# A transformer block on one core: two x tiles on ScalarE's queue, low parts on VectorE or GpSimd, and places for single operations

## The chip, the cores and the metric

The kernel is one program on one core of a Trainium2 chip. The metric is the device time of an execution in microseconds (us). The engines are TensorE (PE; its weight loads are listed as PEld), VectorE (DVE), ScalarE (ACT), GpSimd (POOL) and SyncE (SP), which here only issues DMA transfers.

## The reference

Two layers, each added to its input, on 2048 tokens of width 448, in float32:

```python
def layer_1(x, wqkv, wo):                 # S = 2048, D = 448, H = 16 heads of 28
    q, k, v = split(layernorm(x) @ wqkv)
    scores = einsum("bhqd,bhkd->bhqk", q, k) * 28 ** -0.5
    mask = (i - j >= 0) & (i - j < 256)   # each query sees itself and the 255 before it
    p = softmax(where(mask, scores, -1e9))
    return x + einsum("bhqk,bhkd->bhqd", p, v) @ wo

def layer_2(h, w_gate, w_up, w_down):     # 448 -> 1792 -> 448
    n = layernorm(h)
    return h + (gelu(n @ w_gate) * (n @ w_up)) @ w_down
```

## The kernel before

**Precision.** Each matrix operand of a projection is held as a high part, made on ScalarE (`to_hi`, line 467), and a low part, the rest, made by a subtraction on VectorE or GpSimd (`to_lo`, line 470). A product is three passes of TensorE: high by high, high by low, low by high.

**Layer 1.** The tokens are 16 tiles of 128 (`hres`, loaded at line 603). A tile is normalised (statistics at lines 493 and 495, the norm itself at 545 on VectorE, 522 on ScalarE or 541 on GpSimd), turned by TensorE (line 527) and split into parts (`xT`). Values are made at line 683, queries and keys at line 721; the scores at 831, their row maxima with the mask on VectorE (895), the exponentials on ScalarE (901, into `pp`), the triangle of the mask on GpSimd (907). Line 983 multiplies by the values; the sums are drained by ScalarE (467) and VectorE (1021 to 1023), and the output projection is line 1048, with its weights `wo` loaded at lines 1062 and 1069 and split like the others. Tiles 8 to 15 are turned through DRAM (570, 579, 581).

**Layer 2.** The gate and up products use a Strassen-like scheme: sums of weights are made by `weight_set` (lines 1368 for sums, 467 and 470 for their parts), the products are line 1509, and their results leave PSUM by a copy on ScalarE or VectorE (`copied`, lines 1515 and 1516) and by additions on VectorE (`added`, 1521). A part of it is done in the plain way at lines 1296 and 1308. The second half is line 1585, with weights from `down_set`, added to `hres` at line 1605. In its first half a `seen` (1422 on ScalarE, 1423 on VectorE) reads one element of a PSUM bank, so that the order of the banks is kept.

**Order.** Nothing is scheduled by the compiler. The code adds operations to `Lists`, each with an engine, a cost, a latency and a key; `Lists.run` then plays them through a model of the engines and writes every engine's program in the order in which it started them. At each step it takes, among operations that can start at nearly the same time, the one with the smallest key. The table `PLACE` adds a number to the keys of a unit: "k6" is the split of a set of query and key weights, "ws4" a weight set of layer 2, "q", "v", "o" projections, "s", "m", "p", "a" the stages of attention, "ln" norms, "tx" parts of the normalised tokens, "ds" a set of down weights. Some operations may run on either of two engines (`alts`); the loop chooses.

**DMA.** All loads before are issued by SP's queue in one order. The model of a transfer has one bus that all share. At the start the four first x tiles go out, then the two halves of the first value weights (`pp`, line 662), then the first query and key weights (`raw`, line 692). TensorE fills the wait with transposes of nothing (line 1883) until data is there.

Of the kernel before, what the change touches and what calls it, by code (L numbers as in the profile page):

```python
# [116 lines left out]
}  # L117
HAND = {}
# [11 lines left out]
class Op:  # L130
    __slots__ = ("eng", "cost", "lat", "key", "fn", "deps", "users", "left", "banks", "port", "ready", "start", "fin", "unit", "name",
                 "size", "tag", "mode", "alts", "then", "soft")
# [9 lines left out]
class Lists:  # L142
# [3 lines left out]
    def __init__(self):  # L146
        self.ops, self.seen, self.open, self.all, self.unit = [], {}, {}, {}, None
        self.free_ones = {}

    def op(self, eng, cost, lat, key, fn, r=(), w=(), bank=None, port=False, size=0, tag=None, after=(), part=None, mode=0, alts=None):  # L150
# [10 lines left out]
        o.key, o.unit = key + PLACE.get(self.unit, 0), self.unit  # L161
# [37 lines left out]
    def run(self, allowed, idle):  # L199
# [65 lines left out]
        while n:  # L265
# [28 lines left out]
            if e == "sp":  # L294
                bus = max(bus, t + 1.2) + o.size * (0.003 if t < 15 else 0.0034) + {2: 1.0, 3: 0.5}.get(len(dmas), 0)
                lat = bus + 0.7 - t
                dmas.append(t + lat)
# [1656 lines left out]
```

## Time and profile before

| | |
|---|---|
| time, median of 3 runs | 678.3 us (677.99 to 679.79) |
| the profiled execution | 677.47 us, of which the span 675.8 us |
| TensorE busy | 668.2 us (99%) |
| VectorE busy | 532.1 us (79%) |
| ScalarE busy | 361.9 us (54%) |
| GpSimd busy | 201.8 us (30%) |
| granted clock of TensorE | full in nearly every slice |

Busy time of an engine is what it spent in instructions, as a share of the span. Matmuls are pipelined, so that two of them overlap in the timeline, and a group's time is read from the start of one group to the start of the next. Lines are those of the kernel before; in the changed kernel the same code stands 121 to 123 lines further down.

### The profile page before, as it was taken

To read this page: it belongs to the slowest core of one execution; us is meant where nothing else is said; L and a number is where in the kernel's file an instruction comes from. 1 tells how busy PE (TensorE), PEld (TensorE's weight loads), DVE (VectorE), ACT (ScalarE), POOL (GpSimd) and SP (SyncE) were. 2 spreads that over 40 slices of the span, in tenths; PEclk is the share of its full clock that TensorE was granted. 3 is DMA by queue.
4 is the path that set the end of the run, shared out by engine and by line. 5 is a ranking of instruction groups with operands and counts; after the bars stand their busy time and mean duration, and the time that the engine had idled before them with its cause. 6 is when DMAs were issued, how large, how long until landed. Compare 5 with 4: busy or idle time off the path is not lost.

```text
span 675.8 us, 21887 instructions
## 1 busy us (share of the span) xinstructions
PE 668.2 (99%) x8673; PEld 560.5 (83%) x8673; DVE 532.1 (79%) x1613; ACT 361.9 (54%) x788; POOL 201.8 (30%) x392
## 2 busy tenths in 40 slices
PE   8999999999999999999999999999999999999997
PEld 7887778777877676788888988888899999899887
DVE  8977887977788789469978899668568878887745
ACT  4748777565655475645554475643534445546430
POOL 5125755655555464822121131200000110000000
PEclk9999999999999999999999999999999999999999
DMA  8333231112203265108663964425014734543103
GB/s 300 103 80 85 50 69 46 35 34 64 66 9 68 79 211 179 34 1 222 139 148 93 240 187 143 127 77 157 8 32 129 235 111 128 146 147 89 44 15 110
DMA packets 76678, 71.61 MB, mean 106 GB/s; under 512 B 50080, under 2 KB 64608, under 8 KB 76000
## 3 DMA queue, kind: packets, MB, share of 16 engines
q1 hardware_dynamic: 76432, 70.10, 37.3%
q8 instruction: 68, 1.11, 0.7%
q14 instruction: 34, 0.28, 0.2%
q10 hardware_dynamic: 144, 0.11, 0.0%
HBM read 59.87 MB, written 23.36 MB: 123 GB/s over the span
## 4 chain that ended last, share of the span: by engine, by line
PE 94%; DMA 2%; DVE 1%; ACT 1%; issue 0%; POOL 0%; DVEq 0%; SPq 0%; ACTq 0%
PE bank L1509 27%; PE bank L1585 19%; PE bank L831 11%; PE bank L721 11%; PE bank L1296 7%; PE bank L1048 6%; PE bank L683 6%; PE bank L983 6%; PE bank L1308 2%; DMA proj<-down 1%; PE bank L1621 1%; DMA raw<-in_wo_dram 1%; PE bank L527 0%; DMA hres<-in_x_dram 0%; ACT pp L901 0%
## 5 line engine op out<-in xcount | busy, mean ns | idle before, releaser
L895 DVE CUSTOM_DVE_ANT_0 mt<-bank,mt 128x192 bf16<-128x192 f32 (+4 forms) x368 | 115.1, 373 | 23.3 <-PE bank L831 20.8
L1509 PE MATMUL bank<-xT,proj 64*128 64x512 f32 x645 | 116.7, 389 | 0.2 <-ACT raw L1515 0.2
L907 POOL TENSOR_SCALAR_AFFINE_SELECT pp<-pp 64x256 f32<-64x256 f32 x240 | 96.9, 425 | 58.8 <-ACT pp L901 53.9
L1509 PE MATMUL bank<-xo,proj 64*128 64x512 f32 x456 | 93.1, 388 | 0.4 <-DVE e L1423 0.4
L901 ACT ACTIVATE pp<-bank 128x512 f32<-128x512 f32 x152 | 79.1, 597 | 23.2 <-PE bank L831 23.1
L1509 PEld LDWEIGHTS bank<-xT,proj 64*128 64x128 f32 x645 | 75.5, 184 | 7.5 <-ACT raw L1515 0.6
L721 PE MATMUL bank<-xT 128*128 128x512 f32 x308 | 79.8, 402 | 0.0
L1585 PE MATMUL bank<-proj,gh 64*128 64x448 f32 x624 | 72.1, 362 | 0.0
L721 PEld LDWEIGHTS bank<-xT 128*128 128x128 f32 x308 | 55.4, 188 | 16.1 <-ACT pp L901 2.3
L1585 PEld LDWEIGHTS bank<-proj,gh 64*128 64x128 f32 x624 | 61.3, 184 | 5.0 <-ACT e L1422 0.2
L1509 PEld LDWEIGHTS bank<-xo,proj 64*128 64x128 f32 x456 | 55.7, 184 | 5.7 <-DVE e L1423 0.8
L1509 PE MATMUL bank<-xT,w 64*128 64x512 f32 x276 | 51.1, 388 | 0.0
L1605 DVE TENSOR_TENSOR hres<-bank,hres 128x448 f32<-128x448 f32 (+1 forms) x85 | 47.4, 609 | 2.4 <-PE bank L1621 1.9
L831 PE MATMUL bank<-k,q 28*64 28x320 f32 (+4 forms) x1544 | 46.9, 338 | 0.5 <-ACT pp L901 0.3
L1509 PE MATMUL bank<-xo,w 64*128 64x512 f32 x240 | 46.5, 391 | 0.2
L831 PE MATMUL bank<-q,k 29*64 29x320 f32 (+4 forms) x1472 | 43.7, 350 | 0.0
L683 PE MATMUL bank<-proj,xT 128*128 128x448 f32 (+1 forms) x220 | 43.0, 337 | 0.4 <-ACT proj L467 0.3
L831 PEld LDWEIGHTS bank<-q,k 29*64 29x64 f32 x1472 | 27.3, 131 | 18.3 <-issue 7.3
L683 PEld LDWEIGHTS bank<-proj,xT 128*128 128x128 f32 x220 | 35.5, 189 | 5.4 <-issue 1.0
L831 PEld LDWEIGHTS bank<-k,q 28*64 28x64 f32 x1544 | 35.4, 131 | 5.1 <-DVE mx L895 1.3
L983 PE MATMUL bank<-pp,v 64*29 64x192 f32 (+4 forms) x1472 | 38.6, 340 | 0.6 <-ACT pp L901 0.6
L1296 PE MATMUL bank<-xT,proj 64*128 64x512 f32 x312 | 37.8, 390 | 0.0
(200 smaller groups left out, 1275.1 us busy)
## 6 DMA issues: line engine op xcount, KB each, us to landing
gu<-in_gu_dram SPq DMA_DIRECT2D x18, 480.0 KB
proj<-gu SPq DMA_DIRECT2D x24, 288.0 KB
proj<-down SPq DMA_DIRECT2D x22, 224.0 KB
proj<-gu SPq DMA_DIRECT2D x24, 192.0 KB
hres<-in_x_dram SPq DMA_DIRECT2D x16, 224.0 KB
w<-gu SPq DMA_DIRECT2D x12, 288.0 KB
out_dram<-hres SPq DMA_DIRECT2D x15, 224.0 KB
xT<-xn SPq DMA_DIRECT2D x26, 128.0 KB
```

Source lines behind the costliest of these rows:

```text
L683: op("pe", mm(224 * n), 0.29 if n == 1 else 0.38, key + a / 16, lambda a=a, h=h, wb=wb, xb=xb: nc.tensor.matmul(bank[b.k][:, 0:224 * n], x ...
L721: op("pe", mm(512) + 0.002, 0.403, key, lambda a=a, h=h, wb=wb, xb=xb: nc.tensor.matmul(bank[b.k], wqk[m][:, h, wb, :], xT[:, xb, cc * 128 ...
L831: nc.tensor.matmul(bank[banks[j].k][dst, at:at + 64 * n], w, x, start=True, stop=True, tile_position=(32 * j, 64 * h), skip_group_check=True)
L895: nc.vector.tensor_tensor_reduce(junk[turn_of[0]][:, 0:x], bank[b.k][:, 64 * o:64 * o + x], mask[:, lo:lo + x], 1.0, -BIG, OP.add, OP.max, ...
L901: op("act", 0.065 + width * 0.00088, 0.16 + width * 0.00088, key, lambda: nc.scalar.activation(pp[:, j, at:at + width], bank[b.k][:, 0:wid ...
L907: nc.gpsimd.affine_select(a, a, pattern=[[0, 4], [-cm, 64]], compare_op=op_, fill=0.0, base=0, channel_multiplier=cm)
L983: nc.tensor.matmul(bank[banks[h].k][32 * j:32 * j + DH + 1, 64 * lo:64 * hi], v[HALF[h], at_v(4 * c - 2 + kh // 2), 4 * g + j, :], pp[HALF ...
L1048: op("pe", mm(D), 0.38, wk, lambda a=a, h=h, oh=oh, wh=wh, i=i, k=k: nc.tensor.matmul(bank[k.k][:, 0:D], ohl[h][oh][:, i * 128:(i + 1) * 1 ...
L1296: nc.tensor.matmul(bank[banks[side ^ ph].k], cwbuf[n % 4][0]()[HALF[side], o:o + 128], carea(c, xl, j, side), start=not ph and not j and n ...
L1509: nc.tensor.matmul(bank[b.k], w, xarea(u.cp, xl, xs, side)[:, xk], start=p in (1, 2, 5) and not k and not t, stop=t == 2, tile_position=(6 ...
L1585: nc.tensor.matmul(bank[banks[q].k][:, 0:D], h[oh][0]()[HALF[x], q * 128:q * 128 + 128], d[wh][0]()[HALF[x]], start=not ph and not y and n ...
L1605: op("dve", 0.07 + w * 0.463 / D, 0.163 + w * 0.463 / D, key, lambda: nc.vector.tensor_tensor(hres[:, t, c0:c0 + w], bank[b.k][:, c0:c0 + ...
```

## The change

The changed kernel computes the same with the same number of matmuls. It has five parts. (1) Tiles 2 and 3 of x are loaded by ScalarE's DMA queue in place of SP's; the planner is told that they follow the identity matrix, though no instruction waits for it. (2) The low parts of the value weights and of the query and key weights may run on VectorE or on GpSimd. (3) `PLACE` grows from 163 entries to 866, of which 709 name a single operation ("q0.2:13" is the 13th of unit "q0.2"). (4) `HAND` pins 162 of the operations with a free choice to one engine (75 GpSimd, 62 VectorE, 25 ScalarE), and `DELAY` makes the planner hold 119 single operations back by 0.2 to 1.75 us. (5) The model of a DMA counts ScalarE's transfers on the same bus and lets a third one cost 0.3 us where it was 1.0 and then 0.5.

```diff
 PLACE = {
+    "q0.0:13": -7, "ln1.5n:4": 40, "q0.3": -1, "q0.2:13": 12, "v2.0:7": 7.6, "q0.2:15": 30, "q0.3:16": -16, "q0.4": -17, "ln1.14": 24,
...
 }
-HAND = {}
+HAND = {
+    "k0#1": "pool", "kv1#2": "pool", "k4#1": "pool", "q0.3#1": "dve", "k6#1": "pool", "q0.5#1": "act", "q2.0#1": "dve", "g0#2": "dve",
...
+}
+DELAY = {
...
+    "None:1008": 1.09, "None:1062": 1.16, "None:1073": 0.31,
+}
...
-        o.key, o.unit = key + PLACE.get(self.unit, 0), self.unit
+        self.made[self.unit] = n = self.made.get(self.unit, 0) + 1
+        o.one = f"{self.unit}:{n}"
+        o.key, o.unit = key + PLACE.get(self.unit, 0) + PLACE.get(o.one, 0), self.unit
+        o.delay = DELAY.get(o.one, 0.0)
...
-                bus = max(bus, t + 1.2) + o.size * (0.003 if t < 15 else 0.0034) + {2: 1.0, 3: 0.5}.get(len(dmas), 0)
-                lat = bus + 0.7 - t
+            if o.size:
+                bus = max(bus, t + 1.2) + o.size * (0.003 if t < 15 else 0.0034) + (0.3 if len(dmas) == 2 else 0)
+                lat = bus + 0.7 - t
...
         def load(t, key):
+            if t in (2, 3):
+                op("act", 0.47, 0, key, lambda: nc.scalar.dma_start(hres[:, t, :], xr[t * 128:(t + 1) * 128, :]), ["ident"], [HR(t)],
+                   size=224)
+                return
             dma(key, 224, lambda: nc.sync.dma_start(hres[:, t, :], xr[t * 128:(t + 1) * 128, :]), (), [HR(t)])
...
-            op("dve", 0.54, 0.63, key + 1, lambda b=b: to_lo(wv[:, 1, b:b + 2, n], wv_raw[p][:, b:b + 2], wv[:, 0, b:b + 2, n]),
-               [WVRAW(p, b), WV(p, 0, b)], [WV(p, 1, b)], port=True)
+            arith("dve", 448, key + 1, lambda e, b=b: to_lo(wv[:, 1, b:b + 2, n], wv_raw[p][:, b:b + 2], wv[:, 0, b:b + 2, n], e),
+                  [WVRAW(p, b), WV(p, 0, b)], [WV(p, 1, b)], free_choice=True)
...
-        op("dve", 0.6, 0.7, key, lambda: to_lo(wqk[m][:, 1], wqk_raw[m % 2], wqk[m][:, 0]),
-           [WQKRAW(m % 2), WQK(m, 0)], [WQK(m, 1)], port=True)
+        arith("dve", 512, key, lambda e: to_lo(wqk[m][:, 1], wqk_raw[m % 2], wqk[m][:, 0], e),
+              [WQKRAW(m % 2), WQK(m, 0)], [WQK(m, 1)], free_choice=True)
```

In the two programs as planned, VectorE's additions and subtractions of two tensors fall from 610 to 550 and GpSimd's rise from 103 to 163. Of these 60, 25 are sums of weights (line 1368), 33 are low parts (line 470) and 2 are sums of tokens; 128x384 is the commonest shape (27). The copies out of PSUM at line 1516 (VectorE) rise from 12 to 25, those at line 1515 (ScalarE) fall from 60 to 47, and of the copies of queries and keys VectorE does 6 in place of 1. On TensorE the tile shape (128 by 128 in layer 1's projections, 64 by 32 and 32 by 64 in attention, 64 by 128 in layer 2) changes 129 times in place of 123.

**The start of VectorE's program.** It begins with the statistics of tiles 0 and 1; xn is the norm of tile 0 here. Before:

```order
L493 BN_STATS bnst_75<-hres 128x6
L495 BN_AGGR bnmv<-bnst_75 128x2
L493 BN_STATS bnst_76<-hres 128x6
L495 BN_AGGR bnmv<-bnst_76 128x2
L545 TENSOR_SCALAR xn<-hres,bnmv,bnve 128x448
L493 BN_STATS bnst_75<-hres 128x6
L495 BN_AGGR bnmv<-bnst_75 128x2
L504 SCALAR_TENSOR_TENSOR bnve<-bnmv,bnve 128x1
L493 BN_STATS bnst_76<-hres 128x6
L495 BN_AGGR bnmv<-bnst_76 128x2
L470 TENSOR_TENSOR xT<-bank_151,xT 128x3x128
```

Of the change, over the same stretch (`proj<-pp` is the low part of the first value weights):

```order
L614 BN_STATS bnst_75<-hres 128x6
L616 BN_AGGR bnmv<-bnst_75 128x2
L614 BN_STATS bnst_76<-hres 128x6
L616 BN_AGGR bnmv<-bnst_76 128x2
L614 BN_STATS bnst_75<-hres 128x6
L666 TENSOR_SCALAR xn<-hres,bnmv,bnve 128x448
L616 BN_AGGR bnmv<-bnst_75 128x2
L591 TENSOR_TENSOR proj<-pp,proj 128x2x224
L625 SCALAR_TENSOR_TENSOR bnve<-bnmv,bnve 128x1
L614 BN_STATS bnst_76<-hres 128x6
L616 BN_AGGR bnmv<-bnst_76 128x2
L591 TENSOR_TENSOR xT<-bank_151,xT 128x3x128
```

The norm of tile 0 now stands behind the statistics of tile 2, and the small step that the norm of tile 1 needs (L504 before, L625 now) behind the low part of the value weights.

ScalarE's program at the start, where `proj<-pp` is the high part of the first value weights and bank_151 holds the turned tile 0. Before:

```order
L522 ACT_TABLE_LOAD
L522 ACTIVATE xn<-hres,bnve 128x448
L467 ACTIVATE xT<-bank_151 128x4x128
L467 ACTIVATE proj<-pp 128x2x224 x2
L467 ACTIVATE xT<-bank_150 128x4x128
L522 ACTIVATE xn<-hres,bnve 128x448
```

Of the change:

```order
L725 DMA hres<-in_x_dram 128x448 x2
L588 ACT_TABLE_LOAD
L588 ACTIVATE proj<-pp 128x2x224
L643 ACTIVATE xn<-hres,bnve 128x448
L588 ACTIVATE xT<-bank_151 128x4x128
L588 ACTIVATE proj<-pp 128x2x224
L588 ACTIVATE xT<-raw 128x512
```

The two loads of x stand first and wait for nothing, and the high part of the value weights has moved ahead of the norm of tile 1 and of the high part of tile 0.

**SP's queue around the fourth load of the output weights** (`raw<-in_wo_dram`, the second of the two in these rows). Before:

```order
L1069 DMA raw<-in_wo_dram 128x448
L933 DMA q_163<-mt 1x4x128 x4
L734 DMA k_160<-k_161 4x512
L570 DMA xl_138<-xn 32x14x32 x4
L731 DMA k_161<-k_158 4x512 x4
L1069 DMA raw<-in_wo_dram 128x448
L579 DMA xT<-xl_138 128x3x128
```

Of the change:

```order
L691 DMA xl_138<-xn 32x14x32 x2
L1056 DMA q_163<-mt 1x4x128 x4
L857 DMA k_160<-k_161 4x512
L691 DMA xl_138<-xn 32x14x32 x2
L1192 DMA raw<-in_wo_dram 128x448
L702 DMA xT<-xl_138 128x128
L700 DMA xT<-xl_138 128x3x128
L854 DMA k_161<-q_162 4x512 x4
L1056 DMA q_164<-mt 1x4x128 x4
L691 DMA xl_139<-xn 32x14x32 x4
L854 DMA k_161<-k_158 4x512 x4
```

The four small `k_161<-k_158` transfers, which stood directly ahead of that load, now stand behind it.

**VectorE in a stretch of layer 2**, between two groups of additions to `hres`: sums and low parts of a weight set for later, then the two additions into `v` (L1521 before, L1644 now) that free PSUM banks for TensorE's next products. Before:

```order
L1423 COPY e_74<-bank_151 1x1
L1368 TENSOR_TENSOR xn<-proj,xn 64x384
L1368 TENSOR_TENSOR xn<-proj 64x384
L470 TENSOR_TENSOR proj<-proj 128x384
L1368 TENSOR_TENSOR xn<-proj 64x128
L470 TENSOR_TENSOR proj<-xn,proj 128x384 x2
L1368 TENSOR_TENSOR xn<-proj 128x384
L470 TENSOR_TENSOR proj<-proj 128x256
L1368 TENSOR_TENSOR xn<-proj,xn 128x384
L470 TENSOR_TENSOR e_4869<-v,e_4868 128x512
L1521 TENSOR_TENSOR v<-bank_145,v 128x512
L1521 TENSOR_TENSOR v<-bank_146,v 128x512
```

Of the change, from the start of the same stretch:

```order
L1491 TENSOR_TENSOR xn<-proj 128x384
L1491 TENSOR_TENSOR xn<-proj,xn 128x384
L1491 TENSOR_TENSOR xn<-proj 64x384
L1491 TENSOR_TENSOR xn<-proj,xn 64x384
L1639 COPY v<-bank_147 128x512
L591 TENSOR_TENSOR proj<-xn,proj 128x384
L591 TENSOR_TENSOR proj<-proj 128x384
L1644 TENSOR_TENSOR v<-bank_145,v 128x512
L1644 TENSOR_TENSOR v<-bank_146,v 128x512
L1546 COPY e_74<-bank_148 1x1
L591 TENSOR_TENSOR e_4871<-v,e_4870 128x512
```

Ahead of the two additions stood three more rows than are shown and these ten; now seven rows stand there, and the low part of `e` stands behind them.

## Rows read from the trace of the kernel before

**Rows 1.** The page: busy us by engine (share), instructions.

```profile
PE 668.2 (99%) x8673; PEld 560.5 (83%) x8673; DVE 532.1 (79%) x1613; ACT 361.9 (54%) x788; POOL 201.8 (30%) x392
```

**Rows 2.** Stretches start:end, length; busy PE, PEld, DVE, ACT, POOL; clock, DMA share, GB/s.

```profile
0.00:5.00 5.00, 3.38 (x15) 2.94 (x16) 3.44 (x8) 0.99 (x1) 3.54 (x14) 1.00 0.57 163
5.00:10.00 5.00, 4.63 (x32) 4.15 (x31) 4.02 (x11) 3.58 (x8) 2.77 (x6) 1.00 0.99 312
```

**Rows 3.** The chain, first 10 us: start, length, what.

```profile
0.81 2.58 DMA hres<-in_x_dram
...
3.41 0.64 DVE bnst L493
...
5.27 0.51 DVE xn L545
...
7.95 0.47 ACT proj L467
...
8.47 0.48 PE bank L683 x2
```

**Rows 4.** One more stretch, columns as in rows 2.

```profile
3.00:4.00 1.00, 1.00 (x7) 0.96 (x6) 0.68 (x2) 0.00 (x0) 0.56 (x4) 1.00 0.99 262
```

**Rows 5.** TensorE's waits: us in total, times, longest.

```profile
PE bank L983 <- ACT pp L901: 0.6, 1, 0.6
...
PE bank L831 <- DVE raw L1021: 0.2, 1, 0.2
```

**Rows 6.** The chain, 60 to 67 us.

```profile
60.17 3.91 DMA raw<-in_wo_dram
```

**Rows 7.** SP's queue, 56 to 62 us: start, length of the issues.

```profile
57.45 2.61 SPq L731 DMA_DIRECT2D k<-k  x4
```

**Rows 8.** TensorE's timeline, 360 to 370 us: start, length, line, tiles.

```profile
360.78 1.38 PE L1585 MATMUL bank<-proj,e 64*128 64x448 f32 x12
361.99 0.40 PE L1509 MATMUL bank<-xo,w 64*128 64x512 f32 x2
...
364.05 1.39 PE L1585 MATMUL bank<-proj,e 64*128 64x448 f32 x12
365.50 0.50 PE L1509 MATMUL bank<-xo,w 64*128 64x512 f32 x2
...
367.69 1.38 PE L1585 MATMUL bank<-proj,xT 64*128 64x448 f32 x12
369.22 0.73 PE L1509 MATMUL bank<-xo,w 64*128 64x512 f32 x3
```

**Rows 9.** TensorE's timeline, 394 to 397.5 us.

```profile
395.07 1.53 PE L1585 MATMUL bank<-proj,xT 64*128 64x448 f32 x12
396.98 0.73 PE L1509 MATMUL bank<-xo,proj 64*128 64x512 f32 x3 [0.38 <-DVE e L1423]
```

**Rows 10.** TensorE's timeline, 458.5 to 463 us.

```profile
459.91 1.37 PE L1585 MATMUL bank<-proj,xT 64*128 64x448 f32 x12
461.51 0.50 PE L1509 MATMUL bank<-xT,proj 64*128 64x512 f32 x2 [0.23 <-ACT raw L1515]
```

**Rows 11.** VectorE's timeline, 359 to 370 us.

```profile
361.73 0.56 DVE L1368 TENSOR_TENSOR xn<-proj 128x384 f32<-128x384 f32 x1 [0.59 <-DMA proj<-gu]
...
367.88 1.28 DVE L1521 TENSOR_TENSOR v<-bank,v 128x512 f32<-128x512 f32 x2
```

**Rows 12.** The chain, 454 to 462 us.

```profile
454.78 5.19 DMA proj<-down
```

**Rows 13.** The chain at two visits to line 721.

```profile
70.29 2.72 PE bank L721 x11
...
217.14 5.00 PE bank L721 x22
```

**Rows 14.** A group of one shape: busy us, mean ns | idle.

```profile
L470 POOL TENSOR_TENSOR proj<-proj 128x384 fp32r<-128x384 f32 x5 | 5.6, 1129 | 42.1 <-DVE xn L1368 35.7 <-DVE v L1210 6.4
```

**Rows 15.** Line 470 on VectorE: ns min/median/max, first and last start.

```profile
L470 DVE TENSOR_TENSOR proj<-proj x42: 419/616/1118, 260.6 to 646.9; 128x448 fp32r<-128x448 f32 x28, 128x384 fp32r<-128x384 f32 x7, 128x256 fp32r<-128x256 f32 x7
```

More of the change, by code (lines that the diff above doesn't have):

```diff
@@ L130 @@
 class Op:
-    __slots__ = ("eng", "cost", "lat", "key", "fn", "deps", "users", "left", "banks", "port", "ready", "start", "fin", "unit", "name",
-                 "size", "tag", "mode", "alts", "then", "soft")
+    __slots__ = ("eng", "cost", "lat", "key", "fn", "deps", "users", "left", "banks", "port", "ready", "start", "fin", "unit", "name", "one",
+                 "size", "tag", "mode", "alts", "then", "soft", "delay")
 class Bank:
@@ L147, in __init__ @@
         self.ops, self.seen, self.open, self.all, self.unit = [], {}, {}, {}, None
-        self.free_ones = {}
+        self.free_ones, self.made = {}, {}
     def op(self, eng, cost, lat, key, fn, r=(), w=(), bank=None, port=False, size=0, tag=None, after=(), part=None, mode=0, alts=None):
@@ L211, in run @@
         for o in self.ops:
-            o.left, o.ready, o.start = len(o.deps), 0.0, None
+            o.left, o.ready, o.start = len(o.deps), o.delay, None
             for b in o.banks:
@@ L322, in run @@
                 if not u.left:
+                    u.ready += u.delay
                     for x in u.alts or (u.eng,):
@@ L602, in load, with const_ident @@
         def load(t, key):
+            if t in (2, 3):
+                op("act", 0.47, 0, key, lambda: nc.scalar.dma_start(hres[:, t, :], xr[t * 128:(t + 1) * 128, :]), ["ident"], [HR(t)],
+                   size=224)
+                return
             dma(key, 224, lambda: nc.sync.dma_start(hres[:, t, :], xr[t * 128:(t + 1) * 128, :]), (), [HR(t)])
+        def const_ident():
+            nc.gpsimd.memset(ident, 1.0)
+            nc.gpsimd.affine_select(ident, ident, pattern=[[-1, 128]], compare_op=OP.is_equal, fill=0.0,
+                                    base=0, channel_multiplier=1)
+        ident_at = op("pool", 0.55, 0.6, -100, const_ident, (), ["ident"], port=True)
         op("pool", 0.1, 0.1, -101, lambda: nc.gpsimd.memset(nhalf, -0.5), (), ["nhalf"])
@@ L625, in start @@
             load(t, -64 + t)
-        def const_ident():
-            nc.gpsimd.memset(ident, 1.0)
-            nc.gpsimd.affine_select(ident, ident, pattern=[[-1, 128]], compare_op=OP.is_equal, fill=0.0,
-                                    base=0, channel_multiplier=1)
-        ident_at = op("pool", 0.55, 0.6, -100, const_ident, (), ["ident"], port=True)
         op("pool", 0.1, 0.1, -30, lambda: [nc.gpsimd.memset(m, 0.0) for m in mx], (), [("mx", u, n) for u in range(2) for n in range(32)])
```

148 rows, old and new, of tables (DELAY, HAND, PLACE) are left out of this document.

## The prediction

> **What bounds the kernel now.** I read the busy times first: TensorE works 668.2 of the 675.8 us of the span, VectorE 79%, ScalarE 54%, GpSimd 30% [rows 1]. The number of matmuls doesn't change, so the kernel can only gain where TensorE stands still or changes its way of working, and there are some 8 us of that. About 2 of them lie in the first 10 us, where TensorE is busy 3.38 + 4.63 us [rows 2], much of it with transposes of nothing. The chain of the first 10 us shows what the start hangs on: the first x tile lands at 0.81 + 2.58 = 3.39, its norm runs on VectorE at 5.27, the high part of the first value weights on ScalarE at 7.95, and the first product that counts starts at 8.47 [rows 3]. Next I read TensorE's waits [rows 5] and then its timeline around each, because a stall is shown whole only by the distance of two groups.
>
> In layer 2 a group of 12 matmuls at line 1585 is normally followed by line 1509 after 361.99 - 360.78 = 1.21 us. Four times it is later: 1.45 at 365.50, 1.53 at 369.22 [rows 8], 1.91 at 396.98 [rows 9] and 1.60 at 461.51 [rows 10]. That is 0.24 + 0.32 + 0.70 + 0.39 = 1.65 us. The first group after a stall is also about 0.1 longer (0.50 at 365.50 against 0.40 at 361.99 [rows 8]), 0.4 for the four. In layer 1 there are two more: 0.6 at line 983 and 0.2 at line 831 [rows 5], 0.7 and 0.3 with that 0.1 each.
>
> **The change part by part.**
>
> *The four stalls of layer 2.* For the first two, VectorE works through sums and low parts from 361.73 on and comes to the additions that free the banks at 367.88 [rows 11]; TensorE goes on right after them. The order listing shows thirteen rows ahead of these additions before and seven now, two of them copies or low parts that must come first anyway. So these two should go, and the third (again behind a read on VectorE, L1423 [rows 9]) likewise, since the weight sets of that stretch have also lost about half of their rows to GpSimd. The fourth comes from a transfer of down weights that takes 5.19 us from 454.78 [rows 12]: ScalarE stands in front of it, and a copy out of PSUM is queued behind. The changed order issues that load earlier against its use, by about 2 us of matmuls, more than the 0.39 that is lost. I count all four: -2.05 us. If only half of them go, it is -1.
>
> *The output weights.* TensorE waits 0.6 because the fourth load of output weights is issued at 60.17 and lands 3.91 later [rows 6], behind four small transfers that take SP from 57.45 on, 2.61 us [rows 7]. In the changed queue these four stand behind the load. The load is then up to 2.6 us earlier and the wait, 0.6 long, should go: -0.7.
>
> *The wait for the drain at line 831 (0.2 [rows 5]).* After line 983 the old order has the next scores wait for a bank that ScalarE and VectorE drain in turn. The new one puts nine matmuls of line 1308 between two pieces of the scores. -0.3.
>
> *Changes of tile shape.* The price is put together from two visits to line 721: 11 matmuls take 2.72, 22 in one visit 5.00, so two visits of 11 cost 0.44 more than one of 22 [rows 13]. That is 0.22 for a visit, which has two changes of shape, so 0.11 for a change on this side; on the other side it may be as much again. Six changes more: +0.66 to +1.3. I take +0.9.
>
> *Moved operations.* GpSimd gets 60 operations more. A low part of 128x384 takes it 1.13 us [rows 14], VectorE about 0.56 (a sum of that shape [rows 11]; the median of mixed low parts is 0.62 [rows 15]). That is some 60 x 1.1 = 66 us on an engine that is busy 201.8 [rows 1], and it has room. VectorE loses 60 x 0.56 = 34 us and takes 18 copies, 0.64 each like its additions of that size [rows 11], about 12. None of it is on TensorE's path as long as the parts are ready before their set is used. If that cover fails, a part that is late by its longer duration costs about 0.6 each. A conflict in which VectorE is held up is below. I allow +0.3 for new waits of the size of one old one (0.24 to 0.70).
>
> *The start.* Here no row shows two engines issuing. From below: if SP's transfers keep their pace, the first value weights come third in the queue and no longer fifth, their high part fits in before the norm of tile 1, and the first product waits only for the high part of tile 0, which ends at 7.95, when that of the weights starts now [rows 3]: 8.47 becomes about 7.97, -0.5. From above: the DMA engines are already 0.99 busy at 262 GB/s between 3 and 4 us [rows 4], which is 0.87 us for a tile of 229 KB. If tiles 2 and 3 interleave with tiles 0 and 1, tile 1 is complete after four tiles and not two, 1.75 later, at about 3.39 + 0.87 + 1.75 = 6.0 (an estimate). VectorE must then do the statistics of tiles 1 and 2 ahead of the norm of tile 0 (the order listing), 0.64 each, so that this norm starts near 7.4 in place of 5.27 and ends at 7.9. From its end to that of the high part of tile 0 it is now 7.95 - 5.78 = 2.17 [rows 3]; with that the first product comes near 10.1, 1.6 late. Engines that are full favour the upper end, the earlier place of the weights the lower one, so I take the middle, +0.5.
>
> The Trainium skill, DMA: Bandwidth & Descriptors, section "Issuing engines are not separate DMA queues", says that transfers started by different engines run on the same 16 DMA engines and interleave, and that a second issuer only saves issue time. No run here shows it yet; by that rule the start is the upper end, and the sum below would be smaller by 1.1.
>
> **The sum.** +0.5 - 0.7 - 0.3 - 2.05 + 0.9 + 0.3 = -1.35 us on the profiled execution of 677.47. That execution is 0.8 below the median of 678.3, within the spread of the runs shown; I put the same difference on the median: 676.9.
>
> **The rivals.**
>
> *All goes well (faster).* Start -0.5, changes of shape at 0.66, no new wait: -0.5 - 0.7 - 0.3 - 2.05 + 0.66 = -2.9, so 675.4. For it speaks that each of the six waits has a cause which the new order removes; against it that the start has full DMA engines.
>
> *The x tiles interleave.* Start +1.6: the sum is -0.25, so 678.0. For it speaks the share of 0.99 [rows 4].
>
> *The stalls come back elsewhere.* Half of layer 2's stalls go and the rest turn up behind other operations: -0.35, so 677.9. For it speaks that VectorE stays the busiest helper; against it that it loses 34 - 12 = 22 us.
>
> *GpSimd holds VectorE up (slower).* A low part on VectorE with a median of 0.62 has taken up to 1.12 [rows 15], so something holds it at times by 0.5. With 60 more operations of 0.5 to 1.3 us on GpSimd in the stretches where VectorE makes low parts and frees banks, each hit costs TensorE about what an old stall did, 0.41 on average. Three hits above the allowance eat the gain of 1.35, eight make it slower by 0.3%; ten give 676.9 + 4.1 = 681.0. Against it: the old program had 103 such operations, and VectorE's four waits fell where its own queue was long.
>
> The Trainium skill, SBUF — State Buffer, section "Who interferes with whom", says that VectorE and GpSimd share one pair of ports as an exclusive lock for a whole instruction. The longest row of line 470 agrees with that (1.12 against 0.62), though the trace doesn't name the holder.
>
> *The change does little.* Waits that one execution shows may differ in the next; then only the changes of shape are left, +0.9.
>
> **How the numbers follow.** About 0.3% (2 us) is what a measurement of this kernel can tell from no change. I give the forecast, with 676.2 to 677.6 as its own range, a chance of 0.40; it lies just inside that bound, so 0.06 of it counts as faster. All goes well, below 676.2: 0.29, faster. Interleaving or stalls that come back, 677.6 to 678.9: 0.17, no change. GpSimd in the way: 0.12, slower. Little: 0.02, slower or the same. Together 0.35 faster, 0.51 the same, 0.14 slower. The range leaves out 0.1 above, in the slower case beyond 680.0, and 0.1 below, the best part of the good case under 674.8.
>
> **What the profile of the changed kernel would show.** Right: no wait at line 983 near 65 us; distances of 1.2 us between groups of the second half and the next products around 365, 396 and 460; in all some 2 us less in TensorE's waits of layer 2. The start shows in two numbers, the landing of x's second tile and the first value product (8.47 now). Wrong: the first product after 9.5; low parts on VectorE that last above 1 us, more of them than before, followed by waits of line 1509; new waits on GpSimd's sums and low parts; or a busy time of TensorE that grows by more than 1.3 us.

## The result and the profile after

The changed kernel takes 681.06 us (median of 12 runs, 679.98 to 684.81), the one before 678.45 (12 runs): a ratio of 1.004, 95% interval 1.0025 to 1.0056. It is 2.6 us slower; forecast were 1.35 us less, with a range of 674.8 to 680.0. Its profiled execution has a span of 678.3 against 675.8.

The page's first part of the changed kernel answers to [rows 1]: GpSimd has got 67 us more, VectorE lost only 3.

```profile
PE 668.9 (99%) x8673; PEld 549.0 (81%) x8673; DVE 529.5 (78%) x1573; ACT 352.2 (52%) x768; POOL 269.3 (40%) x452
```

TensorE's waits of the changed kernel (total, times, longest) answer to [rows 5]. The wait of 0.6 for the output weights and the two of line 1509 (0.4 for a read, 0.2 for a copy) are gone; other names stand there.

```profile
...
PE bank L1708 <- DVE e L1546: 1.5, 2, 1.3
PE bank L1744 <- DVE hres L1728: 0.6, 1, 0.6
PE bank L1632 <- ACT e L1545: 0.5, 1, 0.5
PE bank L648 <- DVE xn L666: 0.5, 1, 0.5
...
PE bank L954 <- DVE raw L1144: 0.2, 1, 0.2
...
```

To see where each microsecond went, I set the start of the nth matmul of a line in one trace against that in the other, at places where the order inside is the same again. The lag of the changed kernel, worked out so from the two traces:

| at (time before, us) | lag | what lies between |
|---|---|---|
| 56 (scores) | +0.80 | the start |
| 73 | +0.24 | the wait for the output weights is gone: -0.6 |
| 206 | +0.15 | |
| 295 (first part of layer 2) | +0.79 | eight changes of tile shape more (two fewer ahead of it), one wait at 262 less: +0.6 |
| 321 | +0.88 | |
| 352 | +2.79 | new waits at 332 and 340: +1.9 |
| 409 | +1.05 | the stalls at 365, 369 and 397 (and one at 402) are gone: -1.75 |
| 470 | +0.51 | the stall at 461 is gone: -0.5 |
| 483 | +1.32 | new wait near 473 (in the changed kernel's time): +0.8 |
| 655 | +1.39 | |
| last matmul | +2.16 | new wait at the end: +0.7 |
| end of the span | +2.5 | one addition is left behind it: +0.35 |

**The start.** The chain of the first 11 us answers to [rows 3]; below it VectorE's timeline and a line of TensorE's.

```profile
1.26 3.85 DMA hres<-in_x_dram
...
6.99 0.54 DVE proj L591
...
8.45 0.66 PE bank L648 x4
```

```profile
4.14 0.63 DVE L614 BATCH_NORM_STATS2 bnst<-hres 128x6 f32<-128x448 f32 x1 [1.04 <-DMA hres<-in_x_dram]
...
5.13 0.63 DVE L614 BATCH_NORM_STATS2 bnst<-hres 128x6 f32<-128x448 f32 x1
...
6.41 0.50 DVE L666 TENSOR_SCALAR xn<-hres,bnmv,bnve 128x448 f32<-128x448 f32 x1
...
7.45 0.15 DVE L625 SCALAR_TENSOR_TENSOR bnve<-bnmv,bnve 128x1 f32<-128x1 f32 x1
```

```profile
8.93 0.84 PE L806 MATMUL bank<-proj,xT 128*128 128x224 f32 x3
```

Tile 0 is there for its statistics at 4.14 (3.41 before [rows 3]), tile 1 only at 5.13. The norm of tile 0 waits for the statistics of tile 2 and starts at 6.41 (5.27 before [rows 3]). The small step for tile 1 stands behind the low part of the weights (6.99) and runs at 7.45; ScalarE's norm and TensorE's transposes (8.45) follow it, and the first value product starts at 8.93 (8.47 before [rows 3]). That is 0.46; by 56 us the lag is 0.80.

**332 and 340 us.** VectorE's timeline, and below it GpSimd's, in the stretch where TensorE waits twice for a read on VectorE.

```profile
329.84 1.25 DVE L620 TENSOR_SCALAR bnve<-bnmv 128x2 f32<-128x2 f32 x1
...
332.27 1.75 DVE L591 TENSOR_TENSOR xo<-e,xo 128x512 fp32r<-128x512 f32 x1
...
340.34 0.14 DVE L1546 COPY e<-bank 1x1 f32<-1x1 f32 x1
```

```profile
329.34 1.73 POOL L591 TENSOR_TENSOR xT<-raw,xo 128x512 fp32r<-128x512 f32 x1 [9.63 <-ACT xo L588]
...
332.12 1.35 POOL L591 TENSOR_TENSOR xo<-xo 64x512 fp32r<-64x512 f32 x1 [0.20 <-ACT xo L588]
```

A statistics step of 128x2 numbers takes 1.25 us and a low part 1.75, each from about the time at which GpSimd began a low part until that ended (329.34 + 1.73 = 331.07; 332.12 + 1.35 = 333.47) and its own work was done. Undisturbed they take 0.15 and 0.67 (a run below shows both). Behind them VectorE works without a break until 340.34, where it does the read that TensorE waits for.

**473 us.** In the chain of this stretch ScalarE comes to a high part that waits for a small load (`mhl`); a copy out of PSUM and a read of a bank stand behind it, and TensorE behind those.

```profile
468.35 4.12 DMA mhl<-rest
...
472.71 0.15 ACT v L1638
...
473.19 0.15 ACT e L1545
473.34 0.73 PE bank L1632 x3
```

The kernel before had the same load at nearly the same place (SP's and ScalarE's timelines), but the copy ahead of the high part:

```profile
467.84 0.45 SPq L1389 DMA_DIRECT2D mhl<-rest  x1
```

```profile
471.12 0.60 ACT L1515 ACTIVATE v<-bank 128x512 f32<-128x512 f32 x1 [1.39 <-PE bank L1509]
472.11 0.31 ACT L467 ACTIVATE mhl<-mhl 64x128 fp32r<-64x128 f32 x1 [0.39 <-DMA mhl<-rest]
```

The load went out at 467.84 and now at 468.35, which is the lag at this place (0.51) and no more. So the load is not later against TensorE's work; what is new is that the high part stands in front of the copy.

**The end.** TensorE's last matmul, and VectorE's additions around it.

```profile
674.08 0.37 PE L1744 MATMUL bank<-w,gh 128*128 128x224 f32 x1 [0.55 <-DVE hres L1728]
```

```profile
673.64 0.39 DVE L1728 TENSOR_TENSOR hres<-bank,hres 128x224 f32<-128x224 f32 x1 [0.61 <-PE bank L1744]
674.49 0.92 DVE L1728 TENSOR_TENSOR hres<-bank,hres 128x224 f32<-128x224 f32 x2 [0.46 <-PE bank L1744]
```

The two halves of the last tile are added ahead of the tile before it. The last matmul waits for the first half's addition, and the full tile's addition is left behind everything. Before, all nine followed one another without a gap.

### The profile page after: what moved, and what is told of

Its sections match the earlier page's. It is cut to its first block, busy times and chain, and to the rows that moved or that the text cites. A ratio compares the mean times of both kernels' runs of the same rounds, so it can differ in the third digit from the quotient of the medians.

```text
span 678.3 us, 21853 instructions
## 1 busy us (share of the span) xinstructions
PE 668.9 (99%) x8673; PEld 549.0 (81%) x8673; DVE 529.5 (78%) x1573; ACT 352.2 (52%) x768; POOL 269.3 (40%) x452
## 4 chain that ended last, share of the span: by engine, by line
PE 93%; DVE 4%; DMA 1%; ACT 1%; issue 1%; POOL 0%; DVEq 0%; SPq 0%; ACTq 0%; POOLq 0%
PE bank L1632 28%; PE bank L1708 18%; PE bank L954 11%; PE bank L844 11%; PE bank L806 6%; PE bank L1171 6%; PE bank L1419 5%; PE bank L1106 5%; PE bank L1431 2%; PE bank L1744 1%; DVE mt L1018 1%; DMA mhl<-rest 1%; DMA hres<-in_x_dram 1%; PE bank L648 0%; POOL pp L1030 0%
## 5 line engine op out<-in xcount | busy, mean ns | idle before, releaser
L1018 DVE CUSTOM_DVE_ANT_0 mt<-bank,mt 128x320 bf16<-128x320 f32 (+4 forms) x368 | 114.1, 372 | 22.2 <-PE bank L954 14.6
L1632 PE MATMUL bank<-xT,proj 64*128 64x512 f32 x645 | 113.8, 389 | 0.0
L1632 PE MATMUL bank<-xo,proj 64*128 64x512 f32 x456 | 90.7, 388 | 0.0
L1632 PEld LDWEIGHTS bank<-xT,proj 64*128 64x128 f32 x645 | 71.8, 184 | 9.3 <-DVE e L1546 0.3
L1708 PEld LDWEIGHTS bank<-proj,gh 64*128 64x128 f32 x624 | 59.2, 184 | 7.0 <-DVE e L1546 0.6
L1632 PEld LDWEIGHTS bank<-xo,proj 64*128 64x128 f32 x456 | 51.7, 184 | 7.4 <-ACT e L1638 0.3
L591 POOL TENSOR_TENSOR proj<-xn,proj 128x384 fp32r<-128x384 f32 (+1 forms) x19 | 17.5, 922 | 59.7 <-ACT proj L588 48.8
```

Of the source, the lines that this page charges most:

```text
L1018: nc.vector.tensor_tensor_reduce(junk[turn_of[0]][:, 0:x], bank[b.k][:, 64 * o:64 * o + x], mask[:, lo:lo + x], 1.0, -BIG, OP.add, OP.max, ...
L1632: nc.tensor.matmul(bank[b.k], w, xarea(u.cp, xl, xs, side)[:, xk], start=p in (1, 2, 5) and not k and not t, stop=t == 2, tile_position=(6 ...
L1708: nc.tensor.matmul(bank[banks[q].k][:, 0:D], h[oh][0]()[HALF[x], q * 128:q * 128 + 128], d[wh][0]()[HALF[x]], start=not ph and not y and n ...
```

## The experiments

Two ways of making a variant are used. Some replan (a table entry less). In the others the plan of the changed kernel, or of the one before, is kept, and single operations are moved in it or issued on another engine. A lag is that of the run's one trace. `ahead("a", "b")` puts operation a directly ahead of b in the finished order. All ratios are to the kernel before.

### 1. Tiles 2 and 3 by SyncE again

```diff
-                op("act", 0.47, 0, key, lambda: nc.scalar.dma_start(hres[:, t, :], ...
+                op("act", 0.47, 0, key, lambda: nc.sync.dma_start(hres[:, t, :], ...
```

> The changed kernel with tiles 2 and 3 of x issued by SyncE again (x0, x1, x2, first value weights, x3 in its queue); nothing else moves. If the two queues share the transfers and that made tiles 0 and 1 late (4.14 and 5.11 us for the start of their statistics), the statistics of tile 0 start at 3.4 again, the first value product near 8.0 to 8.5 in place of 8.93, and the span falls by 0.5 to 1.0 us from 678.3. If the late start comes from the new order on VectorE and ScalarE, the first product stays near 8.9 and the span does not change.

Measured: 681.67 us, ratio 1.0046 (1.0029 to 1.0063), span 680.3. VectorE's timeline at the start:

```profile
3.45 0.63 DVE L614 BATCH_NORM_STATS2 bnst<-hres 128x6 f32<-128x448 f32 x1 [0.36 <-DMA hres<-in_x_dram]
...
6.10 0.63 DVE L614 BATCH_NORM_STATS2 bnst<-hres 128x6 f32<-128x448 f32 x1 [1.08 <-DMA hres<-in_x_dram]
6.64 0.50 DVE L666 TENSOR_SCALAR xn<-hres,bnmv,bnve 128x448 f32<-128x448 f32 x1
...
8.62 0.15 DVE L625 SCALAR_TENSOR_TENSOR bnve<-bnmv,bnve 128x1 f32<-128x1 f32 x1
```

Neither theory alone: tile 0 is early again (3.45), but tile 2 now lands at 6.10, the norm of tile 0 stands behind it (6.64), and the step for tile 1 moves to 8.62. The lag to the changed kernel is 1.15 at 33 us. With this order on VectorE a late tile 2 makes a late start; ScalarE's queue brings tile 2 earlier (5.89 in the change).

### 2. Two low parts of tokens back on VectorE

```diff
+MOVED = {
+    "tx0.0#12": "dve", "tx0.0#22": "dve",
+}
...
+    for n, (o, _) in enumerate(emits):
+        if o and o.name in MOVED:
+            emits[n] = o, o.ways[MOVED[o.name]][2]
```

> The changed kernel with two low parts of tokens (at 329.3 and 332.1 us on GpSimd) made by VectorE at the same place in the order. Theory 1, GpSimd holds VectorE: two instructions of VectorE that took 1.25 and 1.75 us take 0.15 and 0.68 again, VectorE gets 1.24 us of work more and loses 2.2 of holding, and the waits of line 1708 near 332 and 340 (0.6 and 1.3 us) shrink to below 1 us together; span 677 to 677.6. Theory 2, VectorE's queue is simply too long in the new order: its work grows by 1.24 us, the wait near 340 grows to about 2.5 us, span 679 to 679.6.

Measured: 680.29 us, ratio 1.0027 (1.0016 to 1.0038), span 678.4. VectorE's timeline there:

```profile
331.13 0.15 DVE L620 TENSOR_SCALAR bnve<-bnmv 128x2 f32<-128x2 f32 x1
...
332.46 0.67 DVE L591 TENSOR_TENSOR xo<-e,xo 128x512 fp32r<-128x512 f32 x1
```

VectorE does two operations more and is done earlier: 0.15 and 0.67 for what took 1.25 and 1.75. TensorE's waits for reads on VectorE near 332 and 340 fall from 1.5 to 0.8, and the lag to the changed kernel falls by 0.97 from 322 to 343 us. So theory 1 for the hold, though not for the span. That does not fall because this execution was already 0.7 later at 322 us (0.1 at 33, 0.4 at 200), and another 0.97 is lost between 343 and 384.

### 3. All sums and low parts on the engines they had before

```diff
+MOVED = {
+    "tx0.0#4": "dve", "tx0.0#5": "dve", "ws0#1": "dve", "tx0.0#12": "dve", "tx0.0#22": "dve", "ws0#9": "dve", "tx0.0#18": "dve",
...
+    "ws11#8": "pool", "ws11#9": "pool", "ws16#5": "pool", "ws16#9": "pool",
+}
...
+    for n, (o, _) in enumerate(emits):
+        if o and o.name in MOVED:
+            emits[n] = o, o.ways[MOVED[o.name]][2]
```

> The order of the changed kernel, but every sum and low part with a free choice on the engine that it had before (72 go back to VectorE, 18 to GpSimd). Theory 1: VectorE's held time falls from about 21 us to about 5, the waits near 332 and 340 go, but VectorE has 30 us more of work, so that some waits for it come back; span 676 to 678. Theory 2 (the order alone makes the waits): span 678 to 681, with waits of lines 1632 and 1708 on VectorE of 2 us or more.

Six low parts of layer 1's weights, which had no second engine before, stay on GpSimd. Measured: 683.19 us (four runs, one of them 690.27), ratio 1.0103 (1.0044 to 1.0163), span 680.2. Both theories are half right. From 322 to 350 us the lag to the changed kernel falls by 1.65 (the waits at 332 and 340 are gone), and from 355 to 445 it grows by 3.1: there the new order does worse without GpSimd's help. VectorE's held time (the count is explained in the next section) is 13.8 us and not the 5 expected, so more than half of what the change adds to it comes with the order.

### 4. The engines of the change in the old order

The same edit on the kernel before, with 72 operations to GpSimd and 18 to VectorE.

> The kernel before in its own order, with only the engines of the 90 sums and low parts of the change (72 to GpSimd, 18 to VectorE). Theory 1: VectorE's held time rises from 5 us to 15 or more, and new waits of TensorE on VectorE or GpSimd in layer 2 cost 1 to 4 us, though the waits at 365 and 369 may shrink; span 676 to 680. Theory 2: the moves relieve VectorE and the span falls by 0.6 to 1.3 us, to 674.5 to 675.2.

Measured: 692.3 us, ratio 1.0204 (1.0177 to 1.0232), span 690.0: far outside both expectations. TensorE's waits:

```profile
PE bank L1509 <- DVE v L1521: 1.8, 1, 1.8
...
```

Some 10 us are lost between 370 and 460 us, and VectorE's held time is 26.2 us. GpSimd takes about twice as long for a low part as VectorE (1.13 against some 0.56 for 128x384 [rows 14] [rows 11]). How much of the loss is that and how much the hold was not separated. These engines do badly in an order that was not made for them.

### 5. The kernel before, with tiles 2 and 3 by ScalarE

```diff
+            dma(key, 224, lambda: (nc.scalar if t in (2, 3) else nc.sync).dma_start(hres[:, t, :], ...
```

> The kernel before, with tiles 2 and 3 of x issued by ScalarE and nothing else changed. Theory A, the transfers of the two queues share the engines and that alone delays the start: the statistics of tile 0 start near 4.1 in place of 3.41, the first value product at 8.8 to 9.1 in place of 8.47, the span grows by 0.3 to 0.6 us. Theory B, the new order on VectorE at the start (norm of tile 0 behind the statistics of tile 2, the small step for tile 1 behind the low part of the weights) delays it: here the first value product stays within 0.2 us of 8.47, because the value weights land earlier.

Measured: 679.45 us, ratio 1.0011 (0.9998 to 1.0023), span 677.8. VectorE's and TensorE's timelines:

```profile
4.38 0.63 DVE L493 BATCH_NORM_STATS2 bnst<-hres 128x6 f32<-128x448 f32 x1 [1.28 <-DMA hres<-in_x_dram]
```

```profile
9.44 0.48 PE L683 MATMUL bank<-proj,xT 128*128 128x224 f32 x2 [0.29 <-ACT proj L467]
```

Theory A: tile 0 is ready at 4.38 in place of 3.41, and the first product starts at 9.44 in place of 8.47 [rows 3]. The lag to the kernel before is 1.0 at 27 and at 56 us and 1.2 at 240; another 1.0 comes by 284, which this one execution doesn't explain. The medians differ by 1.1.

### 6. Another order on VectorE at the start

```diff
+    ahead("ln1.1:5", "kv0:2")
+    ahead("ln1.2:1", "ln1.2:3")
+    ahead("ln1.2:2", "ln1.2:3")
```

> The changed kernel with one change of order on VectorE at the start: the norm of tile 0 and the small step for the norm of tile 1 go ahead of the low part of the value weights, and the statistics of tile 2 behind it. Theory B: the first value product moves from 8.93 to 8.3 to 8.6 and the span falls by 0.4 to 0.7 us. Theory A: tiles 0 and 1 land late all the same, the norm of tile 0 gains 0.4 at most, and the first product stays above 8.8.

Measured: 681.7 us, ratio 1.0045 (1.003 to 1.006), span 679.3. TensorE's timeline:

```profile
8.48 0.84 PE L806 MATMUL bank<-proj,xT 128*128 128x224 f32 x3
...
9.98 0.93 PE L806 MATMUL bank<-proj,xT 128*128 128x224 f32 x6 [0.55 <-DVE xT L591]
```

The first product came at 8.48, as theory B has it, but the next wait took more than that: 0.55 for the low part of tile 0, which the moved statistics had put back, and its group starts at 9.98 (9.83 in the change). The lag to the changed kernel is 0.65 at 33 us. A miss.

### 7. The end

```diff
-    "None:1008": 1.09, "None:1062": 1.16, "None:1073": 0.31,
+    "None:1008": 1.09, "None:1073": 0.31,
```

> The changed kernel without the one entry None:1062 of the table of delays. The additions of the last two tiles change places back; the last product should no longer wait for an addition (0.55 us), and nothing should follow the additions of the last tile: the span falls by about 1.0 us. If the tail is late for another reason (the store of the last tile), the span stays within 0.3 us.

Measured: 680.03 us, ratio 1.0023 (1.0011 to 1.0035), span 679.2: 1.0 us below the change by the medians. VectorE's additions are one row again:

```profile
671.33 5.14 DVE L1728 TENSOR_TENSOR hres<-bank,hres 128x448 f32<-128x448 f32 x9 [1.88 <-PE bank L1744]
```

The traced execution has lost 2.0 us to the changed kernel by 670, at waits that the edit does not touch; its span is only 0.9 longer, so the end gains 1.1. One entry of the table of delays cost 1.0 us.

### 8. Five mends at once

The edits of runs 2, 6 and 7, and:

```diff
+    ahead("None:32", "ws0:19")
+    ahead("r7:1", "ws8:2")
```

> The changed kernel with five mends: the order at the start (as in the run on it), the two low parts of tokens back on VectorE, one read of a bank two rows earlier on VectorE near 340 us, the load of the rest weights one place earlier in SP's queue near 468 us, and the last additions in order. If the slowdown is the sum of the five waits that the trace shows (0.5 to 0.9 at the start, 1.9 near 332 and 340, 0.8 near 473, 1.0 at the end), the span falls by 3.5 to 4.5 us to about 674.3 and the kernel is faster than the one before by 0.2 to 0.3%. If waits only move on, the span stays above 676.

Measured: 678.81 us, ratio 1.0011 (0.9993 to 1.0029), span 677.0. The lag to the changed kernel falls by 1.9 from 322 to 343 us, by 0.8 around 473 and by 0.7 + 0.4 at the end, each as the traces had it. Of the first, run 2 has 0.97 by the low parts alone; the rest came with the earlier read. But it is 1.1 later at 33 us and 1.7 at 74, by the order of run 6 and a later landing of tiles 0 and 1 (statistics at 4.33 and 5.39), and 0.85 comes back between 343 and 384 us.

### 9. The same mends with the start of the kernel before

Run 1's edit, the mends of run 8 without the order of run 6, and in its place:

```diff
+    ahead("None:6", "None:7")
+    ahead("ln1.0n:1", "ln1.2:1")
+    ahead("kv0:1", "kv0:3")
+    ahead("ln1.1n:3", "k1:1")
+    ahead("kv0:2", "k1:1")
```

> The changed kernel with the mends of the run before (low parts back, one read earlier, rest load earlier, last additions in order) and with the start of the kernel before: tiles 2 and 3 by SyncE ahead of the value weights, the norm of tile 0 ahead of the statistics of tile 2, the high part of the weights behind that of tile 0. If the loss at the start is the transfers together with that order, the first value product is at 8.4 to 8.6 and followed at once, and the span is 2.5 to 3 us below that of the run with all mends, 674 to 674.5; the kernel is faster than the one before by 0.1 to 0.3%. If the start is bound by something else, the span stays near 677.

Measured: 677.06 us, ratio 0.9988 (0.9976 to 1.0), span 674.7. It is 4.0 us below the change by the medians and 1.2 us below the kernel before measured beside it (678.25), at the edge of what can be told. The lag to the changed kernel falls by 1.86 from 326 to 340 us and by 0.81 around 473. The start is hardly won: the first product is early, but the lag to the changed kernel is only -0.14 at 56 us, and 0.66 to the kernel before stays. The ten products and the transposes behind it are drawn out, 10.75 - 9.21 = 1.54 us against 11.11 - 9.83 = 1.28 in the change. A line of TensorE's timeline, and all its waits that are listed:

```profile
8.51 0.84 PE L806 MATMUL bank<-proj,xT 128*128 128x224 f32 x3 [0.20 <-ACT proj L588]
```

```profile
PE bank L2006 <- DVE bank L762: 1.6, 1, 1.6
PE bank L954 <- DVE raw L1144: 0.2, 1, 0.2
PE bank L844 <- ACT pp L1024: 0.2, 1, 0.2
PE bank L806 <- ACT proj L588: 0.2, 1, 0.2
PE bank L1632 <- ACT e L1638: 0.2, 1, 0.2
```

### 10. Three evictions and reads ahead of high parts on ScalarE

```diff
+    for one in ('ws1:18', 'ws1:10', 'ws1:19', 'ws1:11'):
+        ahead(one, "ws2:14")
+    for one in ('ws2:10', 'ws2:18', 'ws2:11'):
+        ahead(one, "None:120")
+    for one in ('ln2.14n:1', 'tx0.0:56', 'tx0.0:57'):
+        ahead(one, "None:42")
```

> The same with three mends of order on ScalarE near 349, 369 and 379 us: an eviction or a read of a bank goes ahead of the high parts that wait there for sums of weights (from GpSimd or a late transfer). If TensorE's waits there come from ScalarE standing in front of a late sum, the waits near 349, 369 and 380 (0.4 to 0.9 each in three of the runs so far) fall below 0.2, and the span is 0.8 to 1.5 us below that of the run beside it, 673 to 673.5. If VectorE's or TensorE's own order makes them, nothing changes within 0.3 us.

Measured: 681.06 us, ratio 1.0037 (1.0012 to 1.0063), span 680.0. (An eviction is a copy out of a PSUM bank.) A miss: near 348 and 379 us TensorE still waits for ScalarE (0.45 and 0.41), near 372 for a read on VectorE (0.66), and a new wait of 1.6 for an addition stands near 394.

```profile
...
PE bank L1708 <- DVE hres L1728: 1.6, 1, 1.6
...
```

VectorE is held ahead of that addition, in two others of 128x512 that take 0.67 each in run 9:

```profile
386.84 1.50 DVE L1662 TENSOR_TENSOR v<-raw,v 128x512 f32<-128x512 f32 x1
388.26 1.78 DVE L1662 TENSOR_TENSOR v<-e,v 128x512 f32<-128x512 f32 x1
```

Beside them GpSimd makes two sums of tokens, from 386.49 to 389.48. In run 9 the first of the same two sums began while VectorE was at its own, and took 4.03 us in place of 1.29:

```profile
383.67 4.03 POOL L1327 TENSOR_TENSOR e<-xo 128x512 f32<-128x512 f32 x1 [1.02 <-DMA xo<-xn]
```

So the same two engines, a little shifted against each other, gave a hold of 1.9 us on VectorE in one program, and a hold on GpSimd that TensorE did not feel in the other. That the first makes the wait of 1.6 is read from the trace, where VectorE has no break between them; no run tests it.

### 11. Run 9 with the two low parts on GpSimd

Run 9 without the edit of run 2.

> The kernel of the run with all mends and the start of before, but the two low parts of tokens stay on GpSimd as in the change: the cost of the hold in a program without the other waits. If GpSimd holds VectorE, the statistics step and the low part beside them take 1.0 to 1.8 us instead of 0.15 and 0.68, the waits near 332 and 340 come back with 1 to 1.9 us, and the span is 675.7 to 676.6 against 674.7. If the hold is hidden in a program that starts earlier, the span stays within 0.4 of 674.7.

Measured: 678.3 us, ratio 1.0003 (0.9992 to 1.0014), span 676.1, against 677.06 and 674.7 of run 9. VectorE's timeline:

```profile
329.89 1.26 DVE L620 TENSOR_SCALAR bnve<-bnmv 128x2 f32<-128x2 f32 x1
...
332.33 1.73 DVE L591 TENSOR_TENSOR xo<-e,xo 128x512 fp32r<-128x512 f32 x1
```

The same two instructions are long again, 1.26 and 1.73, and the lag to run 9 grows by 0.97 between 326 and 340 us and by 0.2 after it. Two operations of some 1.5 us on GpSimd cost the kernel 1.0 to 1.2 us.

### 12. The start of the kernel before alone

The five lines of run 9 and run 1's edit.

> The changed kernel with the start of the kernel before alone (tiles 2 and 3 by SyncE ahead of the value weights, VectorE's and ScalarE's first rows in the old order). If the start costs what the traces show, the first product is at 8.4 to 8.6, the span falls by 0.2 to 1.0 us from that of the change, and the other waits (332, 340, 473, the end) stay. If an earlier start only makes later waits longer, the span stays at 678.3 or above.

Measured: 680.87 us, ratio 1.0045 (1.003 to 1.0059), span 680.1. The first product is at 8.49, but the lag to the changed kernel is only -0.36 from 33 to 227 us, so that of the 0.80 at 56 us 0.45 stays. It is +0.3 at 271 and +2.0 from 391 on, the most of it near 369 us, where a copy on ScalarE is late:

```profile
PE bank L1632 <- ACT v L1638: 1.1, 1, 1.1
```

## Why the prediction was wrong

**The step that failed** is the allowance of +0.3 for new waits, with the sentence that none of the moved work is on TensorE's path as long as the parts are ready in time. The new waits measured 1.9 + 0.8 + 1.05 = 3.75 us, and some 0.2 elsewhere. With the other terms as measured the sum is 0.8 - 0.6 + 0 - 2.25 + 0.64 + 3.75 + 0.2 = 2.5, the difference of the two spans. Run 9, which takes the three new waits away in the changed program, is no longer slower than the kernel before.

- *GpSimd's operations.* The rival "GpSimd holds VectorE up" gave 681.0, and 681.06 was measured, but not by its count: the agreement is luck. It had ten hits of 0.41; the trace has two at one place that cost 1.9 together with the queue behind them, of which runs 2 and 11 show 1.0 to be the hold. Taken over the whole trace VectorE's instructions that last over 0.25 us longer than the short ones of their shape (the lowest fifth) rose from 9 with 5.2 us in sum (their time over the short ones) to 31 with 20.6. Most are hidden. The number of moved operations alone does not set it: 13.8 with the old engines in the new order (run 3), 26.2 with the new engines in the old order (run 4). I had [rows 15] and called it a rival; as a term of the sum it would have eaten what VectorE gains: I counted 22 us less for it, and its busy time fell by 3.
- *The other new waits* were in no case of mine: on ScalarE a high part that waits for a load, now ahead of a copy that TensorE needs (0.8; issuing that load one place earlier takes the wait away, runs 8 and 9), and a delay on an addition at the very end (1.05, run 7). I had the first mechanism for the old stall at 461 and did not look for a new one of its kind. I looked at the places where the old kernel waited, and not at those where it did not.
- *The start*, +0.5, was 0.8. The steps of its upper end happened, but smaller: statistics of tile 1 at 5.13 (about 6.0 estimated), the norm of tile 0 at 6.41 (7.4), the first product at 8.93 (10.1). The x tiles of two queues share the transfers (run 5: +1.0 in the old order), and VectorE's order puts the norm of tile 0 behind tile 2 (run 1). That accounts for the first product alone: with both undone it is back at 8.51 and 8.49, and still 0.66 and 0.45 stay at 56 us (runs 9 and 12). They come mostly between 9 and 12 us, where TensorE takes products and transposes in another order than before; no run tests that order. The Trainium skill, DMA: Bandwidth & Descriptors, section "Issuing engines are not separate DMA queues", says that they interleave; the traces agree, with statistics of tile 0 at 4.14 and 4.38 in place of 3.41.
- *The stalls of layer 2*, -2.05, came out at -1.75 - 0.5 = -2.25, of which some 0.25 is a stall at 402 that was not in the sum. The size was right. After 461 us, for example, the next products follow as they should, 462.14 - 460.93 = 1.21:

```profile
460.93 1.37 PE L1708 MATMUL bank<-proj,xT 64*128 64x448 f32 x12
462.14 0.40 PE L1632 MATMUL bank<-xT,proj 64*128 64x512 f32 x2
```

  The reason given for this fourth stall was wrong, though. The load of down weights is not issued 2 us earlier against its use: it went out at 454.78 [rows 12] and now goes out at 455.80, with a lag of 1.03 there. ScalarE's order changed. Before, the high part that waits for the load stood ahead of the copy; now the copy goes first (ScalarE's timelines, before and after):

```profile
459.99 0.58 ACT L467 ACTIVATE proj<-proj 128x448 fp32r<-128x448 f32 x1 [2.31 <-DMA proj<-down]
...
460.88 0.58 ACT L1515 ACTIVATE raw<-bank 128x512 f32<-128x512 f32 x1
```

```profile
460.46 0.60 ACT L1638 ACTIVATE raw<-bank 128x512 f32<-128x512 f32 x1 [1.16 <-PE bank L1632]
460.95 0.57 ACT L588 ACTIVATE proj<-proj 128x448 fp32r<-128x448 f32 x1
```

  It is the same swap that costs 0.8 at 473, the other way round.

- *The output weights*, -0.7: -0.6, right.
- *The wait for the drain at line 831*, -0.3: wrong. It is still there (0.2 for the drain at line 1144). The trace has the same scores ahead of it as before; the nine matmuls that I saw in the order stand elsewhere.
- *Changes of tile shape*, +0.9: by the trace eight more lie in the stretch from 206 to 295 us and two fewer ahead of it. The stretch lost 0.64, and 0.3 of an old wait at 262 is gone from it. That fits in size; nothing here separates the changes of shape from the rest of that stretch.

Two slips in the working changed nothing: by its own terms the third rival's sum is -0.30 and not -0.35, and 677.47 lies just below the three runs then shown, not among them.

Moreover the profiled execution is the fastest of the change's 12. In three other traces of nearly the same program (runs 1, 7 and 12) TensorE loses 0.3 to 1.3 us more than in it near 349, 369 and 380 us each. Near 369 it is the landing of one load of weights: VectorE's first sum from it starts at 364.84 in the profiled execution and at 366.59 in run 12, 1.3 later than the lag explains, and the lag then grows by 1.3; in run 7 both are 0.7, in run 1 0.4. Why the load lands later, and what makes the other two waits differ, was not settled; run 10 shows only that the order on ScalarE alone does not cure them.

## What to carry to other kernels

A profile of before shows where a new order will gain, not where it will lose. When a scheduler's order changes everywhere, read the order of after also where nothing waited: the last instructions, and what stands ahead of each bank's release, above all an operation that itself waits for a load. Work moved to GpSimd is charged twice, by its own time and by the time for which VectorE's two-input and even tiny instructions beside it stand still. A plan's engines and its order belong together: run 4, with the new engines in the old order, was 14 us slower than the kernel before, and run 3, with the old engines in the new order, some 2 us slower than the change by the medians of few runs, with intervals that overlap.

## What the hardware showed

A VectorE instruction on 128x2 numbers that takes 0.15 us took 1.25 while GpSimd made a low part of 128x512. The Trainium skill, SBUF — State Buffer, section "Who interferes with whom", has VectorE and GpSimd share a port pair that one instruction holds to its end. The two-input low part (1.75 and 1.73) agrees with that. A step with one tensor input was held as well (1.25 and 1.26, and 0.15 once GpSimd's neighbour was gone).

GpSimd is held too. In run 9 its sum of 1.29 us took 4.03, beside a row of VectorE's instructions with both inputs in SBUF that ended near 386.5. The sum ended at 387.70, about its own 1.2 us after that row, while VectorE went on with additions that read one input from PSUM.
